# Local attention on all 128 rows of TensorE, in a fused attention and expert kernel

## The chip, the cores and the metric

The kernel runs on one core of one Trainium2 chip. The metric is the device time of one execution in microseconds (us). Three runs of the kernel before gave 451.62 to 452.42 us, with a median of 452.07 us.

## What is computed

Three stages follow one another. The change touches the first alone, causal attention for 4 batches, 8 heads, 576 tokens and 64 numbers a head. Heads 0 to 3 are local (a token sees itself and the 31 before it), heads 4 to 7 strided (a token sees every 32nd token before it, and itself).

```python
scores = scale * np.matmul(q, k.transpose(0, 1, 3, 2))
mask_local = (rel >= 0) & (rel < stride)
mask_strided = (rel >= 0) & (pos[None, :] % stride == pos[:, None] % stride)
masks = np.stack([mask_local if h < H // 2 else mask_strided for h in range(H)], axis=0)
scores = np.where(masks[None, :, :, :], scores, -1000000000.0)
scores = scores - np.max(scores, axis=-1, keepdims=True)
attn = np.exp(scores)
attn = attn / (np.sum(attn, axis=-1, keepdims=True) + 1e-09)
return np.matmul(attn, v).astype(np.float32)
```

The second stage is a soft mixture of 8 experts over the 2304 tokens: `logits = x @ phi`, a softmax over the tokens that makes 32 slots out of x, two matrices (`w1`, `w2`) for each expert, and a softmax over the slots that mixes the results back. The third is an MLP, `h = max(x @ w_in, 0)`, `out = (h * h) @ w_out`. `w_in` and `w_out` come as 64-bit floats.

## The kernel before

**Units.** Attention is cut into 16 units of one batch and two heads. Even units are local, odd ones strided (`units`, line 308). A unit passes through these parts: T transposes q and k on TensorE and copies them from PSUM to `qTb` and `kTb` (`st_T`, 446); S adds the mask and multiplies q by k (`st_S`, 496), and VectorE subtracts the row maximum (`less_max`, 487); E is the exponential; PT transposes the probabilities (`st_PT`, 558); A multiplies them by v (`st_AV`, 594); X transposes the result; L multiplies it by `phi` (lines 682 and 688); R1 to R3 keep the running softmax over the tokens, and their matmuls are on line 786.

**A step.** Step u works on unit u (S, E), unit u+1 (T, as Tk and Tq for k and q, in two halves each), unit u-1 (PT, A) and unit u-2 (X). `PIPE` (27) lists the parts of an even and an odd step in order, and `pin` (96) fixes that order on PE, DVE, ACT and POOL. All loads are issued by SP in program order, each behind the one before (`load_to`, 114), and a load that has to wait for its buffer holds back those behind it. At the end of a step `lv` loads v for a later unit, `vd` and `va` (DVE and ACT) copy each local v block one block on, so that 64 keys stand together (`shift_v`, 358), and `ft` fetches two expert weight tiles of 512 KB. Slots in SBUF are few: when the last units are done, the room of attention is given to the weights (`give`, 270).

**A local unit.** The two heads stand in rows 0 to 63 and 64 to 127 of every operand. T takes 64 columns at a time with a plain matmul by the identity (465), 32 matmuls for q and k, and each half is copied by one instruction over 128 rows. S makes 36 matmuls of 64 rows, 32 columns of q and 64 of k (509), one PSUM bank for each head. A makes 40 of 64 rows and 65 columns, the last being ones that give the row sum (605). Two row groups and four column groups of the array are addressed in turn. An fp32 matmul that is not a transpose leaves two records in the trace, one that is a transpose leaves one.

```python
                for h in range(2):
                    nc.tensor.matmul(
                        out=ps[ts(h, 64), ts(r, 72)], lhsT=src[:, ts(8 * h + 4 * i + r, 64)],
                        rhs=ident[0:72, 0:72], start=True, stop=True, tile_position=(0, 64 * h),
                    )
```

v has two buffers for local units (`vLb`, 323), so a local unit's v is asked for four units ahead (887).

**After attention.** Line 1023 is the experts' first layer, 1053 the second; both take weights as they arrive. From line 1176 on the MLP runs, with 1245 as its main line.

Of the kernel before, what the change touches and what calls it, by code (L numbers as in the profile page):

```python
# [31 lines left out]
PAD = 0  # L32

@with_exitstack
def kernel(
# [12 lines left out]
    nc = tc.nc  # L48
# [278 lines left out]
    vS, Ps, Ts = part(128, 2, 8, D), part(128, 8, 2, 64), part(128, 8, 2, 36)  # L327
# [24 lines left out]


    def pad(ps, n=PAD):
        for _ in range(n):
            nc.tensor.matmul(out=ps[:, 384:512], lhsT=identb, rhs=identb, start=True, stop=True)

    def shift_v(u, h, copy):
        vL = vLb[u // 2 % 2]
        copy(vL[64 * h:64 * h + 32, 1:18, 0:D], vL[64 * h + 32:64 * h + 64, 0:17, 0:D])  # L360

    def load_v(u):
# [3 lines left out]
        for h in range(2):  # L366
            src = v[b, 2 * p + h]
            if local(u):
                load_to(
                    vLb[u // 2 % 2][64 * h + 32:64 * h + 64, :, 0:D], src.rearrange("(j p) d -> p j d", p=32)  # L370
                )
# [27 lines left out]
    load_v(2)  # L399
# [8 lines left out]
    nc.vector.memset(kTb[0][:, 0:32], 0.0)  # L408
    diag(ident, [[-1, 128]], 0, 1.0)
    for vL in vLb:  # L410
        nc.vector.memset(vL[:, :, D:D + 1], 1.0)
        for h in range(2):
            nc.vector.memset(vL[ts(2 * h, 32), 0, 0:D], 0.0)
# [26 lines left out]
    behind(nc.gpsimd.memset(Ps, 0.0), last_diag)  # L440
# [5 lines left out]
    def st_T(u, which, halves=(0, 1)):  # L446
# [6 lines left out]
        for i in halves:  # L453
            ps = psum("t")
            if u:
                pad(ps)
            ps = ps[:, 0:288]
            for r in range(4):
                if not local(u):
                    nc.tensor.transpose(  # L460
                        out=ps[:, ts(r, 72)], in_=src[:, ts(4 * i + r, 128)], identity=ident[0:72, 0:72]
                    )
                    continue
                for h in range(2):
                    nc.tensor.matmul(  # L465
                        out=ps[ts(h, 64), ts(r, 72)], lhsT=src[:, ts(8 * h + 4 * i + r, 64)],
                        rhs=ident[0:72, 0:72], start=True, stop=True, tile_position=(0, 64 * h),
                    )
            if local(u):
                o = dst[:, 32 * which:32 * which + S].rearrange("c (p r) -> c p r", r=8)[:, :, ts(i, 4)]  # L470
                ps = ps.rearrange("c (r p) -> c p r", r=4)
            else:
                o = dst[:, ts(i, 288)]
            dve = u == 0 and i
            if which:
                ins = (nc.vector.tensor_copy if dve else nc.scalar.copy)(out=o, in_=ps)  # L476
            elif dve:
                ins = nc.vector.tensor_scalar(out=o, in0=ps, scalar1=scale, scalar2=None, op0=ALU.mult)
            else:
                ins = nc.scalar.activation(out=o, in_=ps, func=AF.Copy, scale=scale)  # L480
            if dve:
                v_first[0] = ins
# [13 lines left out]
    def st_S(u):  # L496
        qT, kT = qTs[u], kTb[u % 2]
        pss = [psum("s") for _ in range(2)]
        m = maskl.rearrange("p t w -> p (t w)") if local(u) else masks.rearrange("p n w -> p (n w)")
        n = m.shape[1]  # L500
        pad(pss[0])
        for ps in pss:
            nc.tensor.matmul(out=ps[:, 0:n], lhsT=identb, rhs=m, start=True, stop=False)
        if local(u):
            P = Pl
            for qb in range(18):
# [7 lines left out]
            for h in range(2):  # L514
                less_max(P[:, :, h], pss[h][:, 0:n].rearrange("p (n w) -> p n w", w=64), 5, 64)
        else:
            P = Ps
            qv = qT.rearrange("c (r h p) -> c r h p", r=8, h=2)
            kv = kT[:, 0:S].rearrange("c (r h p) -> c r h p", r=8, h=2)
# [9 lines left out]
            for a in range(2):  # L529
                less_max(  # L530
                    P.rearrange("p (i a) g w -> p a g i w", a=2)[:, a, :, :, 0:36],
                    pss[a][:, 0:n].rearrange("p (n w) -> p n w", w=36), 8, 36,
# [53 lines left out]
    def norm(dst, src):  # L586
        den = ap_.tile([128, 5], F32, tag="den", name="den", bufs=4)
# [3 lines left out]
            out=dst, in0=src[:, :, 0:D], in1=den[:, :, None].to_broadcast([128, 5, D]), op=ALU.mult  # L591
        )

    def st_AV(u):
        T = ptt[u]
        pss = [psum("o") for _ in range(2)]
        pad(pss[0])
        if local(u):
            vL = vLb[u // 2 % 2]
# [698 lines left out]
```

## Time and profile before

| | |
|---|---|
| median of 3 runs | 452.07 us |
| the profiled execution | 451.3 us |
| its span, first to last instruction | 449.5 us |
| PE busy over the span | 408.5 us (91%) |
| DVE, ACT, POOL busy | 252.5, 242.0, 62.5 us |
| attention, to the first matmul of line 1023 | 0 to 177 us |
| DMA over the span | 156 GB/s |

The last 225 us are the MLP, in which PE is busy 97% of the time. Attention is the uneven part: in the page's 40 slices PE is at 6 to 9 tenths there, and the granted TensorE clock, 1.00 at 2.4 GHz and 0.50 at 1.2 GHz, goes up and down. Before about 50 us that column reads 1.00 only because the trace holds no change of the clock there; how fast matmuls ran is seen from their durations.

### The profile page before, as it was taken

The numbers are of one execution on the slowest core, as the hardware profiler recorded it, in microseconds if no ns is written. First come the engines' busy times: TensorE is split into PE (matmuls) and PEld (weight loads), VectorE is DVE, ScalarE is ACT, GpSimd is POOL, SyncE is SP. The second block draws the span as 40 slices with busy tenths as digits, with TensorE's granted clock in tenths as the row PEclk, the third lists the DMA queues.
The fourth block names the chain that finished last, engine by engine and source line by source line (L and its number), as shares of the span: only waits on it lengthen the run. The fifth ranks groups of instructions, "written<-read, shape, count | busy, mean of one in ns | idle before, by whom it ended". The sixth has DMA issues, their size and how long they took to land.

```text
span 449.5 us, 11728 instructions
## 1 busy us (share of the span) xinstructions
PE 408.5 (91%) x4910; PEld 316.0 (70%) x4910; DVE 252.5 (56%) x538; ACT 242.0 (54%) x532; POOL 62.5 (14%) x85
## 2 busy tenths in 40 slices
PE   7698886998788869999799998999999999999996
PEld 4677764676577555354577886888878888888884
DVE  4344554667445635311677667686867768635344
ACT  1334535265344512101688777766777677766660
POOL 3210100001101000000143114310242113300000
PEclk9999969698978958999999999999999999999999
DMA  7998668399845499999931223231200000003033
GB/s 149 197 215 247 178 189 236 112 253 240 226 153 190 148 412 359 365 410 408 362 97 50 92 93 93 71 117 49 93 0 1 0 2 0 1 1 141 23 117 141
DMA packets 31988, 70.02 MB, mean 156 GB/s; under 512 B 12608, under 2 KB 12864, under 8 KB 31936
## 3 DMA queue, kind: packets, MB, share of 16 engines
q1 hardware_dynamic: 31936, 69.28, 48.9%
q8 instruction: 38, 0.62, 0.6%
q14 instruction: 14, 0.11, 0.1%
HBM read 64.55 MB, written 4.72 MB: 154 GB/s over the span
## 4 chain that ended last, share of the span: by engine, by line
PE 74%; DMA 8%; DVE 7%; issue 5%; ACT 4%; POOL 1%; SPq 0%; DVEq 0%; POOLq 0%; ACTq 0%
PE t L1245 14%; PE s L1245 14%; PE o L1245 13%; DMA w<-in_moe_w_dram 5%; PE t L465 4%; PE t L1201 3%; PE o L617 3%; PE t L460 2%; PE o L786 2%; PE t L578 2%; DMA w<-in_moe_w_out_dram 2%; DMA space<-in_v_dram 2%; PE s L509 2%; PE s L523 2%; PE t L648 2%
## 5 line engine op out<-in xcount | busy, mean ns | idle before, releaser
L1222 DVE TENSOR_TENSOR w<-r,w 128x384 fp32r<-128x384 f32 x95 | 55.4, 583 | 71.8 <-ACT w L1208 71.0
L1245 PE MATMUL s<-w 128*128 128x512 f32 x288 | 83.0, 397 | 0.2 <-DVE part L1260 0.2
L1245 PE MATMUL t<-w 128*128 128x512 f32 x288 | 74.4, 393 | 0.0
L1245 PE MATMUL o<-w 128*128 128x512 f32 x288 | 73.7, 391 | 0.0
L1206 ACT ACTIVATE r<-t 128x384 f32<-128x384 f32 x94 | 46.2, 491 | 42.7 <-PE t L1201 36.7
L1245 PEld LDWEIGHTS o<-w 128*128 128x128 f32 x288 | 54.1, 188 | 12.4
L1245 PEld LDWEIGHTS s<-w 128*128 128x128 f32 x288 | 52.6, 188 | 11.6 <-ACT w L1097 0.6
L1245 PEld LDWEIGHTS t<-w 128*128 128x128 f32 x288 | 53.2, 188 | 10.3
L1207 ACT ACTIVATE r<-r 128x384 f32<-128x384 f32 x94 | 49.5, 526 | 2.9
L1208 ACT CAST w<-r 128x384 fp32r<-128x384 f32 x94 | 48.3, 514 | 3.5
L476 ACT COPY space<-t 128x288 f32<-128x288 f32 x31 | 11.7, 398 | 48.9 <-PE t L465 27.9
L190 POOL TENSOR_SCALAR nm<-w 128x512 f32<-128x512 f32 x28 | 21.2, 762 | 106.2 <-DMA w<-in_moe_w_out_dram 67.7
L1201 PE MATMUL t<-cT,A 128*128 128x384 f32 x96 | 32.3, 338 | 3.1 <-POOL A L1149 1.6
L1098 POOL TENSOR_TENSOR w<-wf,w 128x512 fp32r<-128x512 f32 x16 | 21.7, 1359 | 74.6 <-ACT w L1097 69.7
L465 PE MATMUL t<-ident,space 72*64 72x72 f32 x512 | 28.5, 288 | 1.6 <-DVE xNb L668 0.7
L465 PEld LDWEIGHTS t<-ident,space 72*64 72x64 f32 x512 | 25.6, 189 | 4.8 <-DVE xNb L668 1.9
L554 POOL TENSOR_TENSOR space<-space,sm 128x576 f32<-128x576 f32 x7 | 8.1, 1153 | 120.9 <-DVE sm L553 61.8
L193 DVE TENSOR_SCALAR nm<-nm 128x512 uint32<-128x512 uint32 x32 | 14.4, 449 | 16.8 <-ACT nm L188 10.2
L1201 PEld LDWEIGHTS t<-cT,A 128*128 128x128 f32 x96 | 17.9, 188 | 7.7 <-POOL A L1149 2.0
L194 DVE SCALAR_TENSOR_TENSOR nm<-w,nm 128x512 uint32<-128x512 uint32 x32 | 22.2, 692 | 1.1
L489 DVE TENSOR_REDUCE mx<-s 128x5 f32<-128x320 f32 (+1 forms) x32 | 15.0, 467 | 12.4 <-PE s L523 8.7
L523 PE MATMUL s<-space 64*36 64x36 f32 x512 | 9.0, 229 | 7.9 <-issue 7.9
(203 smaller groups left out, 564.8 us busy)
## 6 DMA issues: line engine op xcount, KB each, us to landing
w<-in_moe_w_dram SPq DMA_DIRECT2D x46, 512.0 KB
space<-in_moe_w_dram SPq DMA_DIRECT2D x18, 512.0 KB
w<-in_moe_w_in_dram SPq DMA_DIRECT2D x16, 512.0 KB
w<-in_moe_w_out_dram SPq DMA_DIRECT2D x16, 512.0 KB
space<-in_k_dram SPq DMA_DIRECT2D x16, 288.0 KB
space<-in_q_dram SPq DMA_DIRECT2D x16, 288.0 KB
out_dram<-part SPq DMA_DIRECT2D x17, 256.0 KB
space<-in_v_dram SPq DMA_DIRECT2D x16, 144.0 KB
```

The costliest lines, as they stand in the source:

```text
L190: nc.gpsimd.tensor_scalar(out=m, in0=hf, scalar1=2.0 ** -112, scalar2=1.0, op0=ALU.mult, op1=ALU.mult)
L194: nc.vector.scalar_tensor_tensor(out=r, in0=hi, scalar=0x80000000, in1=r, op0=ALU.bitwise_and, op1=ALU.bitwise_or)
L465: nc.tensor.matmul(out=ps[ts(h, 64), ts(r, 72)], lhsT=src[:, ts(8 * h + 4 * i + r, 64)], rhs=ident[0:72, 0:72], start=True, stop=True, til ...
L489: nc.vector.tensor_reduce(out=mx[:, 0:n], in_=ps, axis=AX.X, op=ALU.max, negate=True)
L523: nc.tensor.matmul(out=pss[a][64 * h:64 * h + 36, ts(i, 36)], lhsT=qv[ts(a, 64), i, h], rhs=kv[ts(a, 64), i, h], start=False, stop=(i == 7 ...
L1098: nc.gpsimd.tensor_tensor(out=lo, in0=r, in1=hi.bitcast(F32), op=ALU.subtract)
L1201: nc.tensor.matmul(out=ps[:, 0:HB], lhsT=A4[c][:, ts(f % QF, 128)], rhs=cT4[:, c0:c0 + HB], start=True, stop=True)
L1206: nc.scalar.activation(out=r, in_=ps[:, 0:HB], func=AF.Relu)
L1207: nc.scalar.activation(out=r, in_=r, func=AF.Square)
L1208: nc.scalar.copy(out=gh, in_=r)
L1222: nc.vector.tensor_tensor(out=gl, in0=r, in1=gh.bitcast(F32), op=ALU.subtract)
L1245: nc.tensor.matmul(out=acc[t], lhsT=a[:, ts(t, 128)], rhs=wo[f][:, ts(w, 512)], start=(first and k == 0), stop=(last and k == 2),)
```

## The change

For local units both heads are put into one contraction over 128 rows. k is stored as `[128, 2, 608]`: head 0's rows hold zeros in head 1's columns and the other way round, so one matmul of q (128 rows, 32 columns) against 128 columns gives both heads' scores side by side. v becomes `[128, 18, 2, 65]` in the same way. S is then 18 matmuls of 128 columns and A 20 of 130, in four column groups. PSUM banks are split by query tiles (3 and 2) and no longer by head, which makes the DVE work 384 and 256 columns wide where it was 320 and 320. The zeros are written once: `kTb[0]` on DVE, v's halves on POOL.

T of a local unit now uses 128-column transposes as strided units do, 16 of them for q and k. A transpose holds two neighbouring tokens, one above the other, of one head; so each half is copied by two instructions of 64 rows, 8 where there were 4. In unit 0 ACT and DVE take one each.

The zeros double v's tile, and one buffer takes the place of two: v is asked for two units ahead. The strided `Ts` shares the room of the local `Tl`. In both lists of `PIPE` Tk0 and Tk1 now stand ahead of S. `pad`, which made no instruction, is gone.

```diff
 PIPE = (
-    "Rs S Tk0 Tk1 X0 X1 PT0 PT1 Tq0 Tq1 ld E R2 A lv R3 vd va cv ft".split(),
-    "S Tk0 Tk1 L X0 X1 PT0 E PT1 N Tq0 Tq1 ld R1 A lv ft".split(),
+    "Rs Tk0 Tk1 S X0 X1 PT0 PT1 Tq0 Tq1 ld E R2 A lv R3 vd va cv ft".split(),
+    "Tk0 Tk1 S L X0 X1 PT0 E PT1 N Tq0 Tq1 ld R1 A lv ft".split(),
 )
...
-        qTb[u % 2], kTb[u % 2] = part(128, S), part(128, 32 + S)
+        qTb[u % 2] = part(128, S)
+        kTb[u % 2] = part(128, S) if u % 2 else part(128, 2, 32 + S)
...
-            vLb = [part(128, 18, 65) for _ in range(2)]
-            Pl, Tl = part(128, 5, 2, 64), part(128, 5, 128)
+            vL, Pl = part(128, 18, 2, 65), part(128, 5, 2, 64)
...
-    nc.vector.memset(kTb[0][:, 0:32], 0.0)
+    nc.vector.memset(kTb[0], 0.0)
...
-    behind(nc.gpsimd.memset(Ps, 0.0), last_diag)
+    for t in (vL[0:64, :, 1, :], vL[64:128, :, 0, :], Ps):
+        behind(nc.gpsimd.memset(t, 0.0), last_diag)
...
             for r in range(4):
-                if not local(u):
-                    nc.tensor.transpose(
-                        out=ps[:, ts(r, 72)], in_=src[:, ts(4 * i + r, 128)], identity=ident[0:72, 0:72]
-                    )
-                    continue
-                for h in range(2):
-                    nc.tensor.matmul(
-                        out=ps[ts(h, 64), ts(r, 72)], lhsT=src[:, ts(8 * h + 4 * i + r, 64)],
-                        rhs=ident[0:72, 0:72], start=True, stop=True, tile_position=(0, 64 * h),
-                    )
+                nc.tensor.transpose(
+                    out=ps[:, ts(r, 72)], in_=src[:, ts(4 * i + r, 128)], identity=ident[0:72, 0:72]
+                )
             if local(u):
-                o = dst[:, 32 * which:32 * which + S].rearrange("c (p r) -> c p r", r=8)[:, :, ts(i, 4)]
-                ps = ps.rearrange("c (r p) -> c p r", r=4)
+                o = dst[:, i, 32:32 + S] if which else dst
+                o = o[ts(i, 64)].rearrange("c (p r a) -> c a p r", r=4, a=2)
+                io = [(ps[ts(a, 64)].rearrange("c (r p) -> c p r", r=4), o[:, a]) for a in range(2)]
...
-                for h in range(2):
-                    nc.tensor.matmul(
-                        out=pss[h][ts(cg, 32), ts(t, 64)],
-                        lhsT=qT[ts(h, 64), ts(qb, 32)], rhs=kT[ts(h, 64), 32 * qb:32 * qb + 64],
-                        start=False, stop=(qb + 4 >= 18), tile_position=(64 * h, 32 * cg),
-                    )
+                i = t >= 3
+                nc.tensor.matmul(
+                    out=pss[i][ts(cg, 32), ts(t - 3 * i, 128)].rearrange("p (h w) -> p h w", h=2),
+                    lhsT=qT[:, ts(qb, 32)], rhs=kT[:, :, 32 * qb:32 * qb + 64],
+                    start=False, stop=(t == 2 or qb + 4 >= 18), tile_position=(0, 32 * cg),
+                )
...
-                for h in range(2):
-                    nc.tensor.matmul(
-                        out=pss[h][ts(cg, 32), ts(t, 65)],
-                        lhsT=T[ts(h, 64), t, ts(cg, 32)], rhs=vL[ts(h, 64), min(qb, 17)],
-                        start=True, stop=True, tile_position=(64 * h, 32 * cg),
-                    )
+                i = t >= 3
+                nc.tensor.matmul(
+                    out=pss[i][ts(cg, 32), ts(t - 3 * i, 130)],
+                    lhsT=T[:, t, ts(cg, 32)], rhs=vL[:, min(qb, 17)].rearrange("p h e -> p (h e)"),
+                    start=True, stop=True, tile_position=(0, 32 * cg),
+                )
...
-                load_v(a1 + (4 if local(a1) else 2))
+                load_v(a1 + 2)
```

Three places show how the order on the engines moves. The first is ACT at the start: the copies of unit 0 (t_166 and t_186 before, t_164 to t_185 now), the v shift (32x17x64) and the first copies of unit 1. Before:

```order
L476 ACT_TABLE_LOAD
L476 COPY space<-t_166 128x72x4
L360 COPY space<-space 32x17x64
L480 ACTIVATE space<-t_186 128x72x4
L476 COPY space<-t_269 128x288
L476 COPY space<-t_275 128x288
```

Now:

```order
L465 ACT_TABLE_LOAD
L465 COPY space<-t_164 64x288
L465 COPY space<-t_171 64x288
L469 ACTIVATE space<-t_178 64x288
L469 ACTIVATE space<-t_185 64x288
L465 COPY space<-t_209 128x288
L355 COPY space<-space 32x17x64
L465 COPY space<-t_215 128x288
```

All of unit 0's copies now stand ahead of the shift, which waits for v; before, the copy of q stood behind it.

The second is PE from step 1 into step 2: q of unit 2 (t_378 and t_388 before, t_340 and t_347 now), A of unit 0, then the scores of unit 2 and k of unit 3. Before:

```order
L465 MATMUL t_378<-ident,space 64x72 x8
L465 MATMUL t_388<-ident,space 64x72 x8
L605 MATMUL o<-space 32x65 x40
L503 LDWEIGHTS identb
L503 MATMUL s<-maskl,identb 128x320
L503 LDWEIGHTS identb
L503 MATMUL s<-maskl,identb 128x320
L509 MATMUL s<-space 32x64 x36
L460 MATMUL t_502<-ident,space 128x72 x4
L460 MATMUL t_508<-ident,space 128x72 x4
```

Now:

```order
L453 MATMUL t_340<-ident,space 128x72 x4
L453 MATMUL t_347<-ident,space 128x72 x4
L601 MATMUL o<-space 32x130 x20
L453 MATMUL t_392<-ident,space 128x72 x4
L453 MATMUL t_398<-ident,space 128x72 x4
L492 LDWEIGHTS identb
L492 MATMUL s<-maskl,identb 128x384
L492 LDWEIGHTS identb
L492 MATMUL s<-maskl,identb 128x256
L499 MATMUL s<-space 32x128 x18
```

The transposes of k now lie between A and the scores, so ACT has them and A to finish its copies of q.

The third is SP's queue at the end of attention: v of the last units (32x18x64 is a local one, 36x512 a strided one), and the first weights that go into attention's room (`space`). Before:

```order
L115 DMA space<-in_v_dram 32x18x64 x2
L115 DMA w<-in_moe_w_dram 128x1024 x2
L115 DMA space<-in_v_dram 36x512 x4
L115 DMA space<-in_moe_w_dram 128x1024 x4
L115 DMA space<-in_v_dram 36x512 x4
```

Now:

```order
L114 DMA space<-in_v_dram 32x18x64 x2
L114 DMA w<-in_moe_w_dram 128x1024 x2
L114 DMA space<-in_v_dram 36x512 x4
L114 DMA space<-in_moe_w_dram 128x1024 x2
L114 DMA space<-in_v_dram 32x18x64 x2
L114 DMA space<-in_moe_w_dram 128x1024 x2
L114 DMA space<-in_v_dram 36x512 x4
```

Each local v is now asked for one step pair later, so that of the last local unit parts the four weight loads.

## Rows read from the trace of the kernel before

**Rows 1.** stretches: busy us of PE, PEld, DVE, ACT, POOL; granted clock, DMA share, GB/s

```profile
12.00:50.00 38.00, 33.18 (x764) 27.79 (x764) 17.26 (x42) 14.05 (x33) 4.51 (x12) 1.00 0.86 206
50.00:152.40 102.40, 85.59 (x2215) 67.32 (x2212) 57.27 (x143) 50.58 (x135) 5.77 (x5) 0.85 0.69 191
152.40:177.00 24.60, 18.68 (x337) 14.56 (x337) 12.52 (x45) 6.03 (x20) 0.00 (x0) 0.78 1.00 390
```

**Rows 2.** the chain that ended last, in order of time: start us, us, what

```profile
2.51 8.16 DMA space<-in_v_dram
...
177.05 5.85 PE o L1023 x40
183.01 9.50 DMA w<-in_moe_w_dram
```

**Rows 3.** groups of instructions by line, 0 to 215 us

```profile
L465 PE MATMUL t<-ident,space 72*64 72x72 f32 x512 | 28.5, 288 | 1.6 <-DVE xNb L668 0.7 <-DMA space<-in_k_dram 0.6
...
L460 PE MATMUL t<-ident,space 72*128 72x72 f32 x128 | 14.1, 267 | 1.8 <-issue 1.8
...
L476 ACT COPY space<-t 128x288 f32<-128x288 f32 x31 | 11.7, 398 | 48.9 <-PE t L465 27.9 <-PE t L460 20.6
```

**Rows 4.** the timeline of PE: start us, busy us, line, output and input

```profile
13.41 2.18 PE L460 MATMUL t<-ident,space 72*128 72x72 f32 x16
...
28.77 1.34 PE L509 MATMUL s<-space 64*32 64x64 f32 x72
...
46.77 1.41 PE L605 MATMUL o<-space 64*32 64x65 f32 x80
...
58.58 2.19 PE L465 MATMUL t<-ident,space 72*64 72x72 f32 x32
...
64.95 1.22 PE L465 MATMUL t<-ident,space 72*64 72x72 f32 x32
66.11 1.04 PE L605 MATMUL o<-space 64*32 64x65 f32 x80
...
69.05 0.72 PE L460 MATMUL t<-ident,space 72*128 72x72 f32 x8
```

**Rows 5.** the same view, one run of L509 later

```profile
90.57 0.72 PE L509 MATMUL s<-space 64*32 64x64 f32 x48 [0.38 <-issue]
```

**Rows 6.** windows of the L682 and L688 instructions alone: us, PE, PEld, granted clock

```profile
60.70:63.45 2.75, 2.75 (x40) 2.27 (x40) 0.50 0.79 288
```

**Rows 7.** windows of PE: us, busy us, granted clock, DMA share, GB/s

```profile
63.70:67.50 3.80, 3.67 (x131) 1.00 0.18 49
...
28.20:37.20 9.00, 9.00 (x168) 1.00 1.04 213
```

**Rows 8.** who waited for whom, PE, 12 to 178 us: total us, times, longest

```profile
PE s L523 <- issue: 7.9, 4, 3.3
PE o L605 <- issue: 3.7, 3, 2.1
...
PE s L509 <- ACT space L480: 2.5, 1, 2.5
```

**Rows 9.** DMA queues on the page: packets, MB, share of 16 engines

```profile
q8 instruction: 38, 0.62, 0.6%
```

**Rows 10.** the timeline of SP's queue: start us, us

```profile
28.29 0.87 SPq L115 DMA_DIRECT2D space<-in_v_dram  x2
...
48.20 1.83 SPq L115 DMA_DIRECT2D space<-in_v_dram  x2
...
54.00 1.60 SPq L115 DMA_DIRECT2D space<-in_v_dram  x4
...
89.47 0.87 SPq L115 DMA_DIRECT2D space<-in_v_dram  x2
...
104.69 0.87 SPq L115 DMA_DIRECT2D space<-in_v_dram  x2
```

**Rows 11.** who waited for whom, all engines, 0 to 178 us

```profile
ACT space L360 <- DMA space<-in_v_dram: 4.2, 1, 4.2
```

More of the change, by code (lines that the diff above doesn't have):

```diff
@@ L350, in load, with shift_v @@
         raw[u] = (tq, tk)
[L354 to L360, printed above, removed]
+    def shift_v(h, copy):
+        copy(
+            vL[64 * h:64 * h + 32, 1:18, h, 0:D], vL[64 * h + 32:64 * h + 64, 0:17, h, 0:D]
+        )
     def load_v(u):
@@ L407 @@
     nc.gpsimd.memset(ident, 0.0)
-    nc.vector.memset(kTb[0][:, 0:32], 0.0)
+    nc.vector.memset(kTb[0], 0.0)
     diag(ident, [[-1, 128]], 0, 1.0)
-    for vL in vLb:
-        nc.vector.memset(vL[:, :, D:D + 1], 1.0)
-        for h in range(2):
-            nc.vector.memset(vL[ts(2 * h, 32), 0, 0:D], 0.0)
+    for h in range(2):
+        nc.vector.memset(vL[ts(h, 64), :, h, D:D + 1], 1.0)
+        nc.vector.memset(vL[ts(2 * h, 32), 0, h, 0:D], 0.0)
     nc.vector.tensor_copy(identb, ident)
@@ L469, in st_T @@
             if local(u):
-                o = dst[:, 32 * which:32 * which + S].rearrange("c (p r) -> c p r", r=8)[:, :, ts(i, 4)]
-                ps = ps.rearrange("c (r p) -> c p r", r=4)
-            else:
[L473 to L480, printed above, removed]
@@ L481, in st_T @@
-            if dve:
-                v_first[0] = ins
+                o = dst[:, i, 32:32 + S] if which else dst
+                o = o[ts(i, 64)].rearrange("c (p r a) -> c a p r", r=4, a=2)
+                io = [(ps[ts(a, 64)].rearrange("c (r p) -> c p r", r=4), o[:, a]) for a in range(2)]
+            else:
+                io = [(ps, dst[:, ts(i, 288)])]
+            for n, (x, o) in enumerate(io):
+                dve = u == 0 and n
+                if which:
+                    ins = (nc.vector.tensor_copy if dve else nc.scalar.copy)(out=o, in_=x)
+                elif dve:
+                    ins = nc.vector.tensor_scalar(out=o, in0=x, scalar1=scale, scalar2=None, op0=ALU.mult)
+                else:
+                    ins = nc.scalar.activation(out=o, in_=x, func=AF.Copy, scale=scale)
+                if dve:
+                    v_first[0] = ins
@@ L498, in st_S @@
         pss = [psum("s") for _ in range(2)]
[L499 to L503, printed above, removed]
         if local(u):
             P = Pl
+            tiles = ((0, 3), (3, 5))
+            for (t0, t1), ps in zip(tiles, pss):
+                nc.tensor.matmul(
+                    out=ps[:, 0:128 * (t1 - t0)].rearrange("p (t h w) -> p t h w", h=2, w=64), lhsT=identb,
+                    rhs=maskl[:, t0:t1, None, :].to_broadcast([128, t1 - t0, 2, 64]), start=True, stop=False,
+                )
             for qb in range(18):
                 cg, t = qb % 4, qb // 4
-                for h in range(2):
-                    nc.tensor.matmul(
-                        out=pss[h][ts(cg, 32), ts(t, 64)],
-                        lhsT=qT[ts(h, 64), ts(qb, 32)], rhs=kT[ts(h, 64), 32 * qb:32 * qb + 64],
-                        start=False, stop=(qb + 4 >= 18), tile_position=(64 * h, 32 * cg),
-                    )
-            for h in range(2):
-                less_max(P[:, :, h], pss[h][:, 0:n].rearrange("p (n w) -> p n w", w=64), 5, 64)
+                i = t >= 3
[3 more added lines that the diff above has]
+                    start=False, stop=(t == 2 or qb + 4 >= 18), tile_position=(0, 32 * cg),
+                )
+            for (t0, t1), ps in zip(tiles, pss):
+                n = 2 * (t1 - t0)
+                less_max(
+                    P[:, t0:t1].rearrange("p t h w -> p (t h) w"),
+                    ps[:, 0:64 * n].rearrange("p (n w) -> p n w", w=64), n, 64,
+                )
         else:
             P = Ps
+            for ps in pss:
+                nc.tensor.matmul(
+                    out=ps[:, 0:288], lhsT=identb, rhs=masks.rearrange("p n w -> p (n w)"), start=True, stop=False
+                )
             qv = qT.rearrange("c (r h p) -> c r h p", r=8, h=2)
-            kv = kT[:, 0:S].rearrange("c (r h p) -> c r h p", r=8, h=2)
+            kv = kT.rearrange("c (r h p) -> c r h p", r=8, h=2)
             for i in range(8):
@@ L590, in norm @@
         nc.vector.tensor_tensor(
-            out=dst, in0=src[:, :, 0:D], in1=den[:, :, None].to_broadcast([128, 5, D]), op=ALU.mult
+            out=dst, in0=src[:, :, 0:D], in1=den[:, :, None].to_broadcast([128, n, D]), op=ALU.mult
         )
@@ L848 @@
     for h in range(2):
-        shift_v(0, h, (nc.scalar.copy, nc.gpsimd.tensor_copy)[h])
+        shift_v(h, (nc.scalar.copy, nc.gpsimd.tensor_copy)[h])
     nc.vector.memset(one1, 1.0)
```

36 lines of the change are left out of this document (18 added, 18 removed).

## The prediction

> **What bounds the kernel now.** I read the stretches first, then the chain of waits in order of time, then the timeline of PE, and last the waits.
>
> In attention PE is the fullest engine: 33.2 of 38.0 us between 12 and 50 us and 85.6 of 102.4 us up to 152 us, with ACT and DVE near half [rows 1]. From 152 us on DMA is full, 390 GB/s at a share of 1.00: weights stream into the room that attention gives up. The chain shows the rest: the first expert matmuls start at 177.05 us, as soon as attention's last result is there, and from 183 us on the chain is weight loads [rows 2]. So time saved in attention counts if both the start of that stream and the 177 us move left; all behind them moves as a block. The local work is nearly all before 152 us.
>
> PE's speed has two levels. L465 takes 2.19 us for 32 records at 58.58 us and 1.22 us at 64.95 us [rows 4]; around the second the granted clock reads 1.00 (2.4 GHz), and around 61 us 0.50 (1.2 GHz) [rows 6, 7]. Up to about 50 us matmuls run at the slow level whatever the column says: 16 L460 in 2.18 us at 13.41 us, where 8 take 0.72 us at 69.05 us [rows 4]. I call the two slow and fast.
>
> **The change, part by part.** The sum is made against the profiled execution, 451.3 us; the median is 0.8 us above it.
>
> *T on PE.* A local unit has 512/8 = 64 records of L465; it will have 128/8 = 16 in the form of L460 [rows 3]. Slow, a half (q or k) goes from 2.19 us to half of 2.18 us, 1.1 us less; fast, from 1.22 to 0.72 us, 0.5 less [rows 4]. After unit 0 the timeline has 14 halves: seven like the one at 58.58 us, six like the one at 64.95 us, one between (counted as fast). 7 x 1.1 + 7 x 0.5 = **11.2 us less**.
>
> *S and A on PE.* S goes from 72 records of 64 columns to 36 of 128, A from 80 of 65 to 40 of 130, on all rows and in four column groups. L682 has that form (128 rows, 32 columns of weights, 128 columns, four groups in turn). A run of it is 32 such records and 8 of L688, which put 64 columns through one group alone and so count double: 48 parts in 2.75 us, 57 ns each, slow [rows 6]. I take half of that, 28.5 ns, for fast. S becomes 36 x 57 = 2.06 us slow and 1.03 fast, A 40 x 130/128 x 57 = 2.32 and 1.16. S took 1.34 us slow [rows 4] and, from 48 records in 0.72 us [rows 5], 1.08 fast; A 1.41 and 1.04 [rows 4]. So S costs 0.7 more slow and nothing fast, A 0.9 and 0.1. In the timeline S ran slow in 4 of 8 units, A in 2 of 8: 4 x 0.7 + 2 x 0.9 + 6 x 0.1 = **5.2 us more**.
>
> Old S barely followed the clock (1.34 against 1.08 us), so what bound it was the count of records, 15 to 18 ns each, and not the columns; that is why giving up row groups can cost so little. The Trainium skill, TensorEngine Tiling (Array Packing), section Performance Considerations, speaks against the change: with a contraction of 64 it counts row tiling as a factor of 2, which this change drops. By that rule S and A would double, and the sum would come out near zero; it is the third rival below.
>
> *PE's stalls.* PE waited 7.9 us before L523 and 3.7 us before L605 for nothing that the profile shows ("issue") [rows 8]. The q8 queue brought 38 packets, 0.62 MB, marked instruction [rows 9]; PE has 4910 matmuls and as many weight loads, and 0.62 MB over 9820 is 63 bytes, so I take q8 for PE's program and these waits for late packets. Of 3316 matmul records between 12 and 177 us (764 + 2215 + 337) [rows 1] the change removes 8 x (48 + 36 + 40), less 48 of unit 0's T that lie earlier, 944 or 28%. 28% of 11.6 is **3.3 us less**; the ends are 0 and 11.6. The Trainium skill, Runtime: NRT & Kernel Launch, section Instruction fetch mechanics, has a program refilled in blocks of 16 KiB and calls the cost mostly hidden: the packet size agrees with 0.62 MB over 38, the 11.6 us do not look hidden. By that rule this term would be zero and the sum 3.3 us smaller.
>
> *Start.* The first scores waited 2.5 us for ACT [rows 8], whose copy of q stood behind the shift of v, itself 4.2 us late [rows 11] because the load of v landed at 10.67 us [rows 2]. Now the copies stand first, and T of unit 0 is 2.2 us shorter. But the shift still holds the last copies of unit 1. Between 2.5 and 4.7 us; I take **3.0 less**, near the lower end. The added memsets run on DVE and POOL while PE still waits for k.
>
> *Clock.* From one odd step's v load to the next, a pair of steps took 19.9 us in the slow part (28.29 to 48.20 us) and 15.2 us at 1.00 (89.47 to 104.69 us) [rows 10]: 4.7 us a pair. Two pairs lie before 50 us. The first L682 run, at 0.50, ends in a rise to 1.00 [rows 6, 7], and so do the two others that begin at 0.50; S and A will have their form. If the clock rises at the first local pair, up to 9.4 us come back; if it doesn't, nothing. I take half, **4.7 less**.
>
> *ACT.* 4 more copies a unit at 0.40 us [rows 3], 1.6 us in each of 7 units. Their cover is ACT's idle time: ACT was busy 64.6 of 140.4 us [rows 1]. S, which needs the copies of q, now has A and Tk between, about 2 us. All of it on the path would be 11 us; I take **1.0 more**.
>
> *v with one buffer.* A local v is asked for when A has freed the buffer and shifted at the end of the next step. From 48.20 to 54.00 us that is 5.8 us [rows 10]. Its 0.29 MB take 0.8 us at 390 GB/s [rows 1], and took 8.16 us behind four other loads at the start [rows 2]. So 0 to 2.4 us a unit, 0 to 16 in all; nearer the low end, since two loads stand ahead, not four: **1.0 more**. A late shift would hold ACT's and DVE's queues and so the next copies and row maxima. On SP, A of unit 12 now holds back two weight loads; they have some 10 us to spare before DMA is full.
>
> Sum: -11.2 + 5.2 - 3.3 - 3.0 - 4.7 + 1.0 + 1.0 = **-15.0**, 436.3 us, and on the median's scale **437 us**.
>
> **The rivals.**
> 1. *The clock stays up from the first pair on.* The other 4.7 us come back, S and A lose their 5.2, T saves less: about 427 us. For it: rows 6 and 7. Against: other stalls remain, and falls came after them. Chance 0.20.
> 2. *Copies and v take the gain.* Half of 11 and half of 16 on the path in place of 2, and no gain of clock: 447 us. For it: ACT's copies stand in one queue with the exponentials. Against: ACT is half idle. 0.16.
> 3. *Full rows stream twice as long.* S and A double: 4 x 1.34 + 4 x 1.08 + 2 x 1.41 + 6 x 1.04 = 18.8 us more and not 5.2: 451 us. Against: the 57 ns of rows 6. This is the Tiling page's rule. 0.06.
> 4. *Slower: PE falls to 1.2 GHz.* Between 28.2 and 37.2 us PE was busy without a gap, mostly with transposes, and stayed slow [rows 7]; T becomes such transposes. Of the 85.6 us busy up to 152 us, at a mean of 0.85, some 55 are fast [rows 1]; each that falls costs one more. If half do, 27 us less the 10 that the other terms save: 469 us. It decides from 10 us of fallen work on. 0.08.
> 5. *The end doesn't follow.* If the weight stream were late for a reason of its own, 452 us. Against: DMA stands at 191 GB/s up to 152 us, half of what it then does. 0.05.
>
> **How the numbers follow.** My forecast has 0.45. The range reaches from 421 (all stalls and both pairs won) to 449 (rival 2); it leaves out rivals 3 to 5 and little else. A measurement can tell 0.2%, 0.9 us. Faster: 0.45 + 0.20 + 0.16 + 0.03 of rival 3, 0.84; same: 0.08; slower: 0.08.
>
> **What would show it.** T of a local unit at 1.0 to 1.1 us a half slow, 0.6 to 0.7 fast; S at 1.0 or 2.1 us; some 30 packets on q8; the first expert matmul near 162 us; the shift not waiting for v after unit 0. It is wrong if S or A take over 3 us, if PE waits for ACT's copies of q, or if the granted clock from 50 to 150 us is below 0.85.

## The result and the profile after

The changed kernel takes 435.74 us (median of four runs, 431.74 to 438.37), the kernel before, run beside it, 451.85 us. The ratio is 0.9625, with a 95% interval of 0.9541 to 0.9710. Medians are of all runs, while ratios, here and below, leave out runs more than 1.5% above the fastest of their kernel. The profiled execution is the longest of the four, 438.37 us, with a span of 436.6 us. Forecast were 437 us and a range of 421 to 449.

First the page of the kernel after: busy time (with its share of the span and the instructions), and the queue that brings the program.

```profile
PE 395.7 (91%) x3918; PEld 302.2 (69%) x3918; DVE 253.2 (58%) x538; ACT 255.7 (59%) x562; POOL 64.8 (15%) x87
...
q8 instruction: 31, 0.51, 0.5%
```

The stretches of [rows 1] again, after (busy us of PE, PEld, DVE, ACT, POOL; granted clock, DMA share, GB/s):

```profile
12.00:50.00 38.00, 29.08 (x629) 22.89 (x629) 19.30 (x48) 21.35 (x50) 4.08 (x11) 0.78 0.96 232
50.00:152.40 102.40, 83.25 (x1647) 64.26 (x1642) 62.46 (x164) 58.67 (x154) 5.78 (x5) 0.87 0.89 243
152.40:177.00 24.60, 23.83 (x163) 11.47 (x161) 9.00 (x28) 5.42 (x14) 0.00 (x0) 0.78 0.85 326
```

DMA's share went from 0.86 to 0.96 up to 50 us and from 0.69 to 0.89 up to 152 us, with 13 and 27% more bytes in each microsecond. PE has less to do in attention: 29.1 of the 38 us, where it was 33.2.

The account of PE from the start to the first expert matmul, before and after (the columns as above):

```profile
0.00:177.00 177.00, 145.40 (x3383) 114.65 (x3384) 91.77 (x252) 73.65 (x191) 14.77 (x35) 0.88 0.78 219
```

```profile
0.00:162.30 162.30, 130.74 (x2388) 99.50 (x2388) 92.54 (x252) 87.34 (x221) 16.94 (x37) 0.84 0.90 242
```

PE worked 14.7 us less, and it stood idle for 31.6 us both times. So the whole gain up to this mark is PE's work. Its waits changed their kind and not their sum: those on "issue" fell from 15.3 to 11.2 us, those on DVE grew from 7.7 to 10.7, and those on ACT, POOL and loads by 1.4 together.

The groups of PE and ACT, 0 to 215 us, answer to [rows 3]:

```profile
L453 PE MATMUL t<-ident,space 72*128 72x72 f32 x256 | 26.9, 256 | 8.0 <-DVE xNb L668 5.9 <-DMA space<-in_q_dram 0.8 <-POOL w L398 0.5
...
L601 PE MATMUL o<-space 128*32 128x130 f32 x320 | 13.0, 307 | 3.0 <-issue 1.6 <-DVE space L569 1.0 <-ACT space L568 0.4
L499 PE MATMUL s<-space 128*32 128x128 f32 x288 | 12.0, 303 | 0.8 <-issue 0.5 <-ACT space L469 0.3
...
L521 PE MATMUL s<-space 64*36 64x36 f32 x512 | 7.5, 217 | 3.2 <-issue 3.2
```

All transposes of q and k now stand in one line, L453, at 26.9 us; L465 and L460 together took 42.6. S (L499) takes 12.0 us, where L509 took 9.7, and A (L601) 13.0, where L605 took 10.0.

The chain that ended last, in order of time (start us, us, what), up to the first expert matmul:

```profile
10.02 2.28 PE s L499 x36
12.95 5.73 DMA space<-in_q_dram
18.75 13.01 DMA space<-in_v_dram
31.84 1.11 ACT space L355
38.73 2.33 PE o L601 x40
...
55.56 1.25 PE o L601 x40
57.73 1.22 PE s L499 x36
...
108.90 10.15 DMA space<-in_v_dram
119.08 1.12 ACT space L355
...
162.40 7.80 PE o L1023 x49
```

The last row stood at 177.05 us before [rows 2]: 14.7 us, and the span is 12.9 us shorter. The chain up to there used to be mostly PE; now it runs through the loads of two v, 13 and 10 us from issue to landing. The waits of the engines for v, 0 to 163 us (total us, times, longest), answer to [rows 8, 11]:

```profile
DVE space L355 <- DMA space<-in_v_dram: 15.9, 4, 7.3
ACT space L355 <- DMA space<-in_v_dram: 15.3, 6, 6.4
...
PE t L563 <- ACT space L465: 4.1, 3, 3.1
...
PE s L521 <- issue: 3.2, 1, 3.2
...
PE s L513 <- issue: 3.0, 1, 3.0
...
PE t L682 <- issue: 2.9, 1, 2.9
```

PE itself isn't idle for all of such a wait. Within the first one (18.75 to 31.76 us) it stood 3.0 us on "issue" (L513), and then 3.1 us for ACT's copies (L465), which stood behind the shift; 2.9 us on "issue" (L682) fall into the second.

SP's marks at the loads of a local v, the points of [rows 10] (start us, us):

```profile
18.18 0.90 SPq L114 DMA_DIRECT2D space<-in_v_dram  x2
...
41.11 0.87 SPq L114 DMA_DIRECT2D space<-in_v_dram  x2
...
75.04 0.87 SPq L114 DMA_DIRECT2D space<-in_v_dram  x2
...
93.33 0.87 SPq L114 DMA_DIRECT2D space<-in_v_dram  x2
```

They stood at 28.29, 48.20, 89.47 and 104.69 us. The first mark gains 10.1 us, the pair behind it gives 3.0 of them back (it holds the 13.0 us for v), the next two pairs gain 7.3, the pair from 75 us gives 3.1 back, and the rest to the first expert matmul gains 3.3.

### The profile page after: what moved, and what is told of

Read it like the earlier page. It is cut to its first block, busy times and chain, and to the rows that moved or that the text cites. A ratio compares the mean times of both kernels' runs of the same rounds, so it can differ in the third digit from the quotient of the medians.

```text
span 436.6 us, 9773 instructions
## 1 busy us (share of the span) xinstructions
PE 395.7 (91%) x3918; PEld 302.2 (69%) x3918; DVE 253.2 (58%) x538; ACT 255.7 (59%) x562; POOL 64.8 (15%) x87
## 4 chain that ended last, share of the span: by engine, by line
PE 75%; DMA 8%; DVE 8%; ACT 4%; issue 3%; POOL 1%; SPq 0%; DVEq 0%; POOLq 0%; ACTq 0%
PE t L1245 14%; PE s L1245 14%; PE o L1245 14%; DMA space<-in_v_dram 5%; PE o L1023 4%; PE t L1201 4%; PE t L1053 3%; PE t L453 3%; PE o L786 2%; PE o L601 2%; PE s L499 2%; PE o L617 2%; PE t L576 2%; DMA space<-in_k_dram 1%; DMA space<-in_q_dram 1%
## 5 line engine op out<-in xcount | busy, mean ns | idle before, releaser
L1245 PEld LDWEIGHTS s<-w 128*128 128x128 f32 x288 | 52.7, 188 | 11.5 <-ACT w L1097 0.6
L1245 PEld LDWEIGHTS t<-w 128*128 128x128 f32 x288 | 53.3, 188 | 10.3
L453 PE MATMUL t<-ident,space 72*128 72x72 f32 x256 | 26.9, 256 | 8.0 <-DVE xNb L668 5.9
L453 PEld LDWEIGHTS t<-ident,space 72*128 72x128 f32 x256 | 22.5, 161 | 14.8 <-DVE xNb L668 6.8
L465 ACT COPY space<-t 64x288 f32<-64x288 f32 (+1 forms) x46 | 18.2, 410 | 6.6 <-PE t L453 5.9
L469 ACT ACTIVATE space<-t 64x288 f32<-64x288 f32 (+1 forms) x46 | 18.7, 425 | 5.0 <-PE t L453 4.7
L478 DVE TENSOR_REDUCE mx<-s 128x8 f32<-128x288 f32 (+2 forms) x32 | 14.9, 466 | 6.9 <-PE s L499 5.5
```

The lines of the kernel that those rows point to most:

```text
L453: nc.tensor.transpose(out=ps[:, ts(r, 72)], in_=src[:, ts(4 * i + r, 128)], identity=ident[0:72, 0:72])
L469: ins = nc.scalar.activation(out=o, in_=x, func=AF.Copy, scale=scale)
L1245: nc.tensor.matmul(out=acc[t], lhsT=a[:, ts(t, 128)], rhs=wo[f][:, ts(w, 512)], start=(first and k == 0), stop=(last and k == 2),)
```

## The experiments

Two theories stood against each other after this. **v:** the one buffer of v sets the time now, and without its waits several microseconds more come off. **DMA:** attention has run into the transfers, so that a wait taken away at v comes back at k or q, and parts of the change replace one another. The quoted texts say what was expected before each run. The table gives median, ratio to the kernel before on the same chip with its 95% interval, and from each kernel's one profile the first expert matmul, the first matmul of the MLP (us), and PE's waits on "issue" from 12 to 165 us (before: to 177).

| kernel | us | ratio | expert | MLP | issue |
|---|---|---|---|---|---|
| before | 451.1 to 453.6 | 1 | 177.0 | 217.9 | 15.3 |
| changed | 435.74 | 0.9625 (0.9541 to 0.9710) | 162.4 | 205.0 | 11.2 |
| changed again | 440.92 | 0.9763 (0.9647 to 0.9879) | 164.4 | 205.1 | 9.7 |
| two v buffers | 437.52 | 0.9647 (0.9535 to 0.9759) | 162.0 | 204.2 | 9.3 |
| its control | 435.42 | 0.9648 (0.9555 to 0.9741) | 160.7 | 201.3 | 8.9 |
| k, q behind v | 435.64 | 0.9641 (0.9576 to 0.9706) | 161.7 | 202.4 | 6.5 |
| one weight tile a step | 439.37 | 0.9767 (0.9663 to 0.9871) | 150.9 | 208.0 | 4.2 |
| before, new T | 439.64 | 0.9772 (0.9663 to 0.9881) | 167.1 | 207.2 | 17.6 |
| changed, old T | 438.08 | 0.9721 (0.9618 to 0.9824) | 164.0 | 203.4 | 6.2 |
| before, one v buffer | 447.95 | 0.9913 (0.9857 to 0.9969) | 175.2 | 216.2 | 14.9 |
| old order | 433.38 | 0.9664 (0.9583 to 0.9744) | 155.8 | 195.8 | 8.9 |
| old A | 436.16 | 0.9714 (0.9649 to 0.9779) | 160.9 | 200.8 | 10.8 |
| weight tiles 2, 1 | 433.72 | 0.9674 (0.9605 to 0.9744) | 155.4 | 202.5 | 1.2 |
| the same, two v buffers | 433.37 | 0.9669 (0.9611 to 0.9727) | 150.2 | 200.1 | 7.0 |

The span less the MLP's first matmul is 231.6 us before (449.5 - 217.9), after (436.6 - 205.0), and with one tile a step (439.6 - 208.0). So a profile is decided when the MLP starts. The profiled execution is one of four to ten and not always a middle one, so a few microseconds between two marks can be chance.

**The changed kernel again**, beside the next three.

> The changed kernel once more, beside the three others of this call. Both theories: 0.955 to 0.971 of the kernel before, some 432 to 438 us. A second profile: the waits of the v shift for its load should come again after units 0 and 10, 13 and 10 us from issue to landing.

Both numbers missed: 440.92 us and 0.9763, where 432 to 438 us and at most 0.971 were expected. The intervals of the two comparisons overlap, so the change is worth 2.4 to 3.8%, and no two of the changed forms below are told apart. The long waits came again, at 19.05 us (13.3 us) and at 111.86 us (10.2 us), and PE's account too: 130.9 us of work up to the first expert matmul.

**Two v buffers.** v is asked for a step pair earlier; two weight slots pay for it.

```diff
-RING = 26
-NA = 17
+RING = 24
+NA = 19
...
-            vL, Pl = part(128, 18, 2, 65), part(128, 5, 2, 64)
+            vLb = [part(128, 18, 2, 65) for _ in range(2)]
+            Pl = part(128, 5, 2, 64)
...
-                load_v(a1 + 2)
+                load_v(a1 + (4 if local(a1) else 2))
```

> The changed kernel with two zero-padded v buffers, so that a local v is asked for four units ahead again; room for it from two ring slots, given to attention's space. Theory (the v waits lie on the path): the shift waits for v in unit 0 alone, and 8 to 14 us come back, 420 to 428 us. Rival (DMA is full through attention, so that k and q are late next): within 2 us of the changed kernel.

**The control** has the two slots fewer, and one buffer.

> Control for the kernel with two v buffers: the changed kernel with the same two ring slots given to the space, and one v buffer. Theory: within 2 us of the changed kernel, since the number of weight slots is the same in all. Rival (the ring's size sets the weight stream): 3 to 6 us slower, as 1 MB at 400 GB/s is 2.6 us.

The shift's waits after unit 0 went, as meant: in the control DVE and ACT wait 13.1 and 12.5 us for v, here ACT 1.1 us in unit 0. The ratios are 0.9647 and 0.9648, and 8 to 14 us would have shown. So the theory of v falls. (The control, 435.42 us, lies within 2 us of the first 435.74, as expected, but 5.5 below the repeat beside it.) The chain with two buffers shows what is late instead:

```profile
15.04 6.00 DMA space<-in_k_dram
...
51.52 8.01 DMA space<-in_v_dram
...
79.53 4.73 issue
```

PE's own waits for k and q are 5.8 us here and 2.0 in the control, so a part of the wait for v did come back there. Its idle time up to the first expert matmul is about 32.5 us in both.

**k and q behind v.** In odd steps the loads of k and q move behind that of v.

```diff
-    "Tk0 Tk1 S L X0 X1 PT0 E PT1 N Tq0 Tq1 ld R1 A lv ft".split(),
+    "Tk0 Tk1 S L X0 X1 PT0 E PT1 N Tq0 Tq1 R1 A lv ld ft".split(),
```

> The changed kernel, with the load of q and k in odd steps issued behind that of v and no longer ahead of it. The local v then has 0.6 MB less ahead of it on SP's queue, some 2.5 us at 230 GB/s. Theory: the shift's waits shorten by 2 to 3 us where they are long, 429 to 434 us. Rival (q and k become late in its place, as they now wait for A): 434 to 440 us.

DVE's and ACT's waits for v shrink from 15.9 and 15.3 to 10.5 and 8.6 us, and the time stays, as the rival had it. Again a shorter wait for v bought nothing that can be measured. The rival's reason shows only faintly: PE's waits for k and q are 2.6 us, where they were 1.2.

**One weight tile a step** in place of two, in attention.

```diff
-                fetch(2)
+                fetch(1)
```

> The changed kernel, fetching one expert weight tile a step and no longer two, so that attention shares DMA with some 7 MB less. It still loads everything, only later. Theory (attention is now held by DMA, which stands at 225 GB/s and a share of 0.92 between 12 and 132 us): the first expert matmul comes before 155 us where it came at 162 to 164, and the waits of the v shift fall under 10 us on each engine. Rival (attention is held by its own chain of PE, ACT and DVE): 160 to 164 us. In both the whole is slower or the same, 436 to 452 us, since 7 MB at 400 GB/s are 18 us of stream behind attention.

This is the test of DMA. Windows of the changed kernel, then of this one, with its account up to the first expert matmul:

```profile
50.00:100.00 50.00, 40.38 (x800) 30.88 (x794) 33.99 (x86) 32.70 (x88) 3.47 (x3) 0.90 0.96 227
```

```profile
50.00:100.00 50.00, 41.76 (x798) 31.60 (x798) 33.29 (x85) 32.42 (x86) 3.46 (x3) 0.90 0.56 162
```

```profile
0.00:150.90 150.90, 123.75 (x2392) 94.44 (x2395) 92.59 (x252) 87.17 (x221) 16.93 (x37) 0.89 0.70 205
```

The DMA share falls from 0.96 to 0.56, and with the same work on every engine the first expert matmul comes at 150.9 us, 11.5 us earlier. In six profiles with two tiles a step (the changed kernel twice, two v buffers, its control, k and q behind v, and the old order below) the mark lies between 155.8 and 164.4 us. So fewer weights move it by 5 to 13 us: their transfers stretched attention. But the waits that a late load brings, in PE or through the other engines, aren't directly where the time came from. Against the changed kernel PE's work is 7.0 us shorter with the same matmuls, at a mean granted clock of 0.89 for 0.84, and its stalls on "issue" are 7.0 us shorter, while its other waits are some 2.5 us longer. How far the clock follows from the shorter waits for v (6.2 and 5.9 us, under 10 as expected) isn't shown. The kernel before wasn't run with one tile a step, so what the transfers cost it already isn't known. The MLP starts 3.0 us later all the same, since the weights now come behind attention. The chain of this kernel:

```profile
129.31 8.68 DMA w<-in_moe_w_dram
138.00 11.69 DMA w<-in_moe_w_dram
149.71 10.20 DMA space<-in_moe_w_dram
...
200.92 8.02 DMA w<-in_moe_w_in_dram
```

From 129 us on it is weight loads only. Attention isn't on the path at all there, and what it saved is lost.

**The kernel before with the new T alone.** S, A, v and the order stay.

```diff
-                for h in range(2):
-                    nc.tensor.matmul(
-                        out=ps[ts(h, 64), ts(r, 72)], lhsT=src[:, ts(8 * h + 4 * i + r, 64)],
-                        rhs=ident[0:72, 0:72], start=True, stop=True, tile_position=(0, 64 * h),
-                    )
+                nc.tensor.transpose(
+                    out=ps[:, ts(r, 72)], in_=src[:, ts(4 * i + r, 128)], identity=ident[0:72, 0:72]
+                )
```

> The kernel before with the new T alone: 128-column transposes and two copies of 64 rows a half; scores, products with v, order and v buffers as before. Theory (T is the larger part of the gain): 440 to 446 us, and the granted clock as before, with no rise before 40 us. Rival (the form of S and A, and the clock that rises with them, make the gain): 447 to 452 us.

Alone it takes off 2.3%; 439.64 us lie just under the range of the theory. And it does that at 1.2 GHz from 12 to 42 us (a window of this kernel):

```profile
12.00:42.00 30.00, 21.25 (x425) 18.36 (x424) 12.59 (x29) 14.98 (x37) 2.07 (x2) 0.50 0.96 213
```

DMA stands at 0.96 there too: with only T shortened, attention already meets the transfers early on (from 50 to 152.4 us the share is 0.79).

**The changed kernel with the old T**: the diff above the other way round, with the copies that belong to it.

> The changed kernel with the old T: 64-column matmuls by the identity, q copied by one instruction a half and k by two. Theory: 5 to 11 us slower than the changed kernel, 441 to 447 us, and S and A as in the changed kernel. Rival (S, A and the clock make the gain, T is hidden): 433 to 439 us.

It takes 438.08 us: the theory's 441 to 447 us missed, and the rival's range holds. So in the changed kernel T is worth little, and without it the change is still worth 2.8% (1.8 to 3.8). The halves, new T alone (2.3%) and all but the new T (2.8%), would add to 5.1%; the whole gave 3.8% and, in the repeat, 2.4%. Each has a margin of about 1%, so this alone shows only weakly that they replace one another. PE's account up to the first expert matmul shows it better, first with the new T alone, then with all but the new T:

```profile
0.00:167.10 167.10, 131.37 (x2999) 102.28 (x2999) 92.32 (x254) 87.10 (x221) 14.92 (x35) 0.78 0.84 232
```

```profile
0.00:164.00 164.00, 140.40 (x2773) 109.38 (x2774) 92.45 (x251) 79.52 (x206) 16.99 (x37) 0.83 0.85 239
```

The marks stand 9.9 and 13.0 us earlier than before, and with both halves 14.7 (12.6 in the repeat). Putting the new T into the second kernel takes 9.7 us of work from PE and adds 8.0 us of idle time (23.6 to 31.6), 5.0 of them on "issue" and 3.1 on ACT, whose copies stand behind the shift of v. The DMA shares and the experiment on the weights speak for the transfers as the reason; why PE stands on "issue" stays open.

**The kernel before with one v buffer**, asked for two units ahead.

```diff
-            vLb = [part(128, 18, 65) for _ in range(2)]
+            vLb = [part(128, 18, 65), part(128, 18, 65)][0:1] * 2
...
-    load_v(2)
...
-                load_v(a1 + (4 if local(a1) else 2))
+                load_v(a1 + 2)
```

> The kernel before with one v buffer for local units, asked for two units ahead, and nothing else. Theory (one buffer costs little where DMA has slack, share 0.69 between 50 and 152 us): within 4 us of the kernel before, 449 to 456 us. Rival (the shift's wait is on the path): 8 us or more slower, over 460 us.

At 447.95 us it lies 1 us under the theory's range: 0.9% faster (0.3 to 1.4) than the kernel before, not slower. Its shift never waits for v after unit 0: where DMA isn't full (a share of 0.78 from 12 to 50 us), v is there in time. One buffer costs nothing by itself. That the gain comes from the smaller first burst of loads is likely, but wasn't tried apart.

**The old order**: S ahead of the transposes of k, all else changed.

```diff
-    "Rs Tk0 Tk1 S X0 X1 PT0 PT1 Tq0 Tq1 ld E R2 A lv R3 vd va cv ft".split(),
-    "Tk0 Tk1 S L X0 X1 PT0 E PT1 N Tq0 Tq1 ld R1 A lv ft".split(),
+    "Rs S Tk0 Tk1 X0 X1 PT0 PT1 Tq0 Tq1 ld E R2 A lv R3 vd va cv ft".split(),
+    "S Tk0 Tk1 L X0 X1 PT0 E PT1 N Tq0 Tq1 ld R1 A lv ft".split(),
```

> The changed kernel with S ahead of the transposes of k again, as it stood in a step before; all else as changed. Theory 1 (attention now runs into a full DMA, so the order on TensorE hardly counts): 434 to 441 us, ratio to the kernel before 0.962 to 0.978, and the first expert matmul at 160 to 166 us. Theory 2 (the order is what lets scores start without waiting for the copies of q): S waits for ACT's copies again by 1 to 3 us a local unit, 442 to 448 us, first expert matmul at 168 us or later.

The new order is worth nothing that can be measured: 0.9664, and S waits for ACT's copies only 1.8 us in all, so theory 2 falls. The time, 433.38 us, and the first expert matmul lie under the ranges of theory 1; but the 155.8 us are of an execution at 429.2 us, the lowest of six.

**The old A**: 40 matmuls of 64 rows and two v buffers as before; S, T and the order changed.

```diff
-                    lhsT=T[:, t, ts(cg, 32)], rhs=vL[:, min(qb, 17)].rearrange("p h e -> p (h e)"),
-                    start=True, stop=True, tile_position=(0, 32 * cg),
+                        lhsT=T[ts(h, 64), t, ts(cg, 32)], rhs=vLb[u // 2 % 2][ts(h, 64), min(qb, 17)],
+                        start=True, stop=True, tile_position=(64 * h, 32 * cg),
```

> The changed kernel with the old product with v (80 matmuls of 64 rows a local unit, two v buffers of the old form, so no padding in v); S, T and the order as changed. Theory 1 (DMA full): A costs TensorE 3.0 us less, DVE's and ACT's shift no longer waits for v, and the time stays within 434 to 440 us, ratio 0.962 to 0.975, because loads of k or q are late instead. Theory 2 (A on all rows is what costs, by its work and by its single buffer): 425 to 432 us.

A costs 10.3 us on PE in place of 13.0, the shift no longer waits for v after unit 0, and the time stays: 0.9714. Neither PE's 3 us nor the buffer show. But the reason given by theory 1 isn't seen: PE waits 0.9 us for k and not for q. What its trace has is a granted clock of 0.72 from 50 to 100 us, where the changed kernel has 0.90, and 43.0 us of work there in place of 40.4.

**Weight tiles 2, 1**: two fetched in even steps, one in odd steps, behind the load of v.

```diff
-                fetch(2)
+                fetch(2 - u % 2)
```

> The changed kernel, with one weight tile in place of two fetched in each odd step, right behind the load of v; two in even steps as before. Theory 1 (the time after the change is set by DMA: weights in attention are paid by late v, k and q, weights behind it by the expert stage): between the two ends, 2 a step (first expert matmul 162 us, MLP from 205 us) and 1 a step (151 us, MLP from 208 us), there is a better one: first expert matmul at 154 to 159 us, MLP from 199 to 203 us, 430 to 435 us, ratio 0.952 to 0.966. Theory 2 (the sum of bytes alone counts): 436 to 441 us as with either end.

**The same with two v buffers**, the edit of the second experiment.

> As the one before, and two padded v buffers for one, paid with two weight slots. Theory 1 (DMA): with the weights thinned out the wait for v is no longer passed on to k and q, so two buffers now help where they did not before: 1 to 4 us faster than one buffer under the same fetches, 427 to 433 us. Theory 2 (a wait for v is never on the path): the same within 1 us, or slower by the two slots, 431 to 438 us.

In the first of the two the first expert matmul comes at 155.4 us and the MLP at 202.5, both where the theory of DMA put them, and 433.72 us lie in its range; the ratio, 0.9674, lies just outside, and no better version can be told from the changed kernel. Its chain, past 155 us, shows the balance:

```profile
155.59 10.09 DMA space<-in_moe_w_dram
165.75 10.61 DMA w<-in_moe_w_dram
176.42 10.16 DMA space<-in_moe_w_dram
186.60 8.96 DMA w<-in_moe_w_out_dram
```

In this stage the chain is weight loads at a DMA share of 1.03 and 409 GB/s. PE is about as full: up to the MLP it is busy for 42.9 of 47.1 us, and in the changed kernel for 41.4 of 42.6. Two v buffers gave 433.37 us and 0.9669, so the expected 1 to 4 us did not come, and theory 2 holds.

Of the theory of DMA two things are borne out: the weights' transfers stretch attention, and the parts of the change don't add. That a wait taken away at v comes back at k or q is seen in part with two v buffers, and not with the old A.

## Why the prediction was right, and where it was not

The total was right: 437 us forecast, 435.74 measured, and the 14.7 us at the first expert matmul are nearly the sum of -15.0. The repeat, 440.92 us, lies in the range too. The agreement is partly luck. The forecast had PE's work shrink by 8.2 us (T 13.4 with unit 0, S and A 5.2 back) and put the rest on shorter waits and the clock. Measured, PE's work shrank by 14.7 us and its idle time not at all.

- **T: right in its mechanism, 2.3 us short.** -15.7 us on PE, where -11.2 after unit 0 and -2.2 in unit 0 were forecast. Eight records take 1.17 to 1.22 us slow and 0.67 to 0.76 fast, for 1.09 and 0.72; the surplus is that fewer ran slow.
- **S and A: right in sum, not in its parts.** +5.3 us (2.3 and 3.0) for a forecast of 5.2. A run of S takes 2.35 us slow and 1.28 to 1.29 fast, for 2.06 and 1.03; A 2.40 and 1.31 to 1.32, for 2.32 and 1.16. So a run costs up to a quarter more than was forecast, and it came out because more of them ran fast: S ran slow in one unit and partly in another, A in one and partly in two. Rival 3 fell. The Trainium skill's factor of 2 for row tiling (TensorEngine Tiling (Array Packing), Performance Considerations) is nearly met at 1.2 GHz (2.35 to 1.34 us, 1.75) and far from it at 2.4 GHz (1.29 to 1.08, 1.19).
- **PE's stalls: agrees in size, its reason not shown.** All stalls on "issue" went from 15.3 to 11.2 us, 27% down, and the packets of q8 from 38 to 31, as forecast. The forecast took two lines alone, and these went from 11.6 to 4.8 us; other lines stalled in their place. And the new T alone has 35 packets and 17.6 us, and with one and the same program the stalls went from 11.2 to 4.2 and 1.2 us when fewer weights moved. The count of records alone is not what sets them. The lowest two stand where the weights were thinned, but the last kernel has 7.0 us, and with all weights they range from 6.2 to 11.2 us in the changed forms; one profile each doesn't settle it.
- **Start and clock: right in direction; the split isn't shown.** The first scores start at 9.95 us, 2.2 earlier (they started at 12.14), for a forecast of 3.0, and 64 records of L521 take 0.79 us at 13.97 us, the speed of 2.4 GHz, which before came only at about 50 us (at 1.2 GHz they take 1.19, at 28.88 us). The first mark gained 10.1 us. Then came the 13.0 us for v. Windows of the changed kernel, from the start of that wait:

```profile
18.75:26.60 7.85, 5.78 (x131) 4.58 (x130) 3.75 (x10) 4.32 (x12) 1.16 (x1) 1.00 0.97 237
...
26.60:43.70 17.10, 10.64 (x154) 7.89 (x157) 7.80 (x19) 7.22 (x16) 1.15 (x1) 0.50 0.95 232
```

  PE was busy for 5.78 of 7.85 us, and then the granted clock fell to 0.50 (1.2 GHz) for 17 us. So the clock rose in the first pair and was lost again in the next: that the term of one half fits is luck, and the 10.1 us also hold the shorter T and a stall of 2.5 us that the kernel before had at L523.
- **v and ACT: mis-sized.** v was set at 0 to 16 us, 1.0 taken, with 8.16 us as the longest load; the longest took 13.0. The shift waited 15.9 us (DVE) and 15.3 (ACT, 0.9 of it in unit 0), where the sign of being right was "the shift not waiting for v after unit 0". What was said of a late shift came true: it held ACT's copies, and PE waited 4.1 us for them before L563. In all, PE's waits other than on "issue" grew by some 4 us, for the 2.0 of the two terms. Yet two buffers or another order of loads gave nothing back that can be measured, so the wait for v isn't a price that can simply be taken off.
- **Rival 5's counter-argument failed.** "DMA stands at 191 GB/s, half of what it then does" was read as room. After the change 227 to 232 GB/s were a share of 0.96, and before it 206 GB/s were already one of 0.86 up to 50 us [rows 1]. The share was the number to read.
- **Rivals 1 and 4** each came in part: the clock rose in the first pair, and it fell again with both long waits for v (0.50 from 118.8 to 125.6 us, at the end of the 10.15 us of the chain). Over 50 to 152.4 us it is 0.87, for 0.85 before. On balance the clock did count: of the 14.7 us of PE's work T, S and A make 10.4, and the other 4 or so are the same matmuls running faster (L617, 512 records, from 11.5 to 10.0 us). Rival 2 named the right waits, but its sum doesn't come out: 13.5 us in place of 2, and no 4.7 from the clock, make 453 us and not 447, and the upper end of the range rested on it. The lower end doesn't come out either: all stalls and both pairs won make 424 us, not 421.
- **The noise was taken too small.** "A measurement can tell 0.2%", but two comparisons of the same two kernels gave 3.8 and 2.4%.
- **The sum as a method: not borne out.** It added the terms as if each were worth its PE time. The runs show each half alone to be worth 2.3 to 2.8% of the 2.4 to 3.8% of the whole, and the new T's 9.7 us on PE to come back as 8.0 us of idle time once the other half is there. PE's gain was larger than forecast (T and the clock), its waits took back what the forecast had hoped to win from them, and the two happened to cancel.

The stated marks of error did not appear: S and A stayed under 3 us, PE waited only 0.3 us for ACT's copies of q before S (L469, in the groups above), and the clock from 50 to 152.4 us was 0.87.

## What to carry to other kernels

When work is taken from the fullest engine, read the DMA share of that very stretch, not its GB/s, and ask at which shortening it reaches 1: near that the parts of this change stopped adding up, and a shorter wait for one load bought nothing that could be measured. Set the engine's work and its idle time up to a common mark side by side, for each kernel: that shows where a gain went, which a total that agrees with the forecast hides. Prefetching for a later stage is not free either: here one tile a step less made attention 11.5 us shorter and the stage behind it 14.5 us longer, so the best place is judged by the start of the last stage that both precede. Test a change's parts alone before crediting them; each half here gave most of the gain.

## What was not expected of the hardware

A DMA share near 1 did not mean a rate near the highest. The DMA view of the changed kernel from 50 to 100 us, and then from 170 to 200 us:

```profile
DMA packets 7153, 11.35 MB, mean 227 GB/s; under 512 B 4016, under 2 KB 4016, under 8 KB 7146
...
DMA packets 3363, 12.29 MB, mean 410 GB/s; under 512 B 373, under 2 KB 373, under 8 KB 3360
```

Over half the packets in attention are under 512 B: 3456 of 256 B and 560 of 4 B. The Trainium skill (DMA: Bandwidth & Descriptors, Why small descriptors are slow) gives a 256-byte packet 27% overhead; 3456 of them are 0.88 MB, 8% of the bytes, so by that page the rate would lose some 3% (an estimate). The trace shows 227 for 410 GB/s. Nor is it a fixed price for each packet. A packet of 4 KB holds its engine for 240 ns on average from 50 to 100 us, and for 162 ns from 170 to 200 us, where nearly all bytes come in such packets. One of 256 B takes 36 ns from 50 to 100 us, 26 ns in the kernel before (share 0.74) and 18 ns with one tile a step (share 0.56). So in these traces a packet holds its engine longer where the share is higher and sizes are mixed; which part of the path makes it so stays open.

The program's own packets travel by DMA too: 31 of 16 KiB in q8 agree with the blocks that the Trainium skill names (Runtime: NRT & Kernel Launch, Instruction fetch mechanics); the Trainium skill calls the cost "mostly hidden" there. PE's 1.2 to 11.2 us on "issue" with that program would speak against it if they are waits for its packets, and no run shows that they are.
